# The test for the fast path by partition and a matmul, and the state's small matmuls in two bursts

## The chip, the cores and the metric

One core of a Trainium2 chip runs the whole program. The metric is the device time of one execution in microseconds; the runs shown are three executions of the kernel before, with their median. The profile is one more execution, taken by the hardware profiler, with a time of its own. Engines are named as the profile names them: PE (TensorE) with PEld for its weight loads, DVE (VectorE), ACT (ScalarE), POOL (GpSimd), SP (the engine that issues most DMAs).

## The reference, cut to what matters

```python
x = A_x                                                   # [1, 2048, 1024], 32 heads of 32
g = sigmoid((x * gate_w).sum(-1, keepdims=True))
# A: linear attention
q, k, v = heads(x @ A_wqkv)
phi = lambda t: where(t > 0, t + 1, exp(t)) + 1e-6
pq, pk = phi(q), phi(k)
kv = einsum("bhsd,bhse->bhde", pk, v)
z = einsum("bhsd->bhd", pk)
a = (einsum("bhqd,bhde->bhqe", pq, kv) / (einsum("bhqd,bhd->bhq", pq, z)[..., None] + 1e-6)) @ A_wo
# B: each position attends to 8 positions, 2 apart, back from its own
q, k, v = heads(x @ B_wqkv)
b = (softmax(masked(q . k[idx]) * 32 ** -0.5) @ v[idx]) @ B_wo
return g * a + (1 - g) * b
```

(`heads` splits into 32 heads; the heads are joined again ahead of each output product.)

## The kernel before

All engines run one static order. `Prog.op` records each operation with its reads, writes, a cost in the planner's units and a priority; `Prog.schedule` lays the operations out engine by engine, always the ready one of lowest priority; `emit` writes that order with semaphores. Each engine works strictly in its order, so an operation that waits holds all behind it on that engine. PSUM has eight banks; `Pool.next` deals them out, and PE may write a bank again when ACT and DVE have read it.

The program goes through these stages:

- `v` of part B, then `k` and `q` of part B for all positions (`kT`, `qT`), up to about 175 us. While they come, `top` keeps a running maximum and minimum of all values in `mx` on DVE.
- `k` of part A: for each of 16 tiles of 128 positions two groups of eight matmuls, and `phi` (ACT exponent L1374, DVE L1375 and L1377) writes `pk`. Between the groups, one in five `slot` calls starts a `fill`: the sliding attention of 114 positions in one burst of small matmuls (L1518 for scores, and in the same burst L1542, probabilities times `v`, of the fill before), then ACT's exponent into `E`, DVE's mask (L1528), reciprocals (L1553) and products into `ao` (L1554), which go out to `oB_hbm` and come back transposed into `qT`.
- `mT`, the product of x with `pk` (L1712), with the other fills between. POOL adds up `z`, which takes a trip of its own through HBM (`zr`, `zb`).
- `state` (L1682): `kvT`, 32 small products of `w` with `mT` by head, each over 8 chunks: 256 matmuls of 128x32 by 32 columns (L1690) in one operation. Then `query` (`pq`, L1745), `fold` (L1730: `kvT` times A's output weights, 16 matmuls of 32x32 tiles, evicted into `ws[5]`, which lies in `kT`), and `scaled` (the division by `den`, L1758 to L1768).
- `output` (L1771): 16 tiles; each half adds part B (`qT` times `Bo` in `ws[0]`) and part A (`aT` times the folded weights) in one bank, which ACT or DVE scale and evict.

The fast path is right only within bounds on the values: the largest |q| or |k| of part B, squared, must be at most 40/32, and a measure of the gate at most 1e17. `mx4` holds for each partition the maximum, the minimum and the gate's measure. `fast_ok` (L1613) turns this into one number, `flag`: it negates the minimum (L1615), sends the 128x3 values to `mx_hbm` (L1617), reads them back as one row of 384 in one partition (L1618), takes the maximum of each kind (L1619) and tests it (L1622 to L1625). Its DVE operations get a priority 40 later than their place. In `tail`, every engine waits for `flag`, loads it and branches to the fast or the general path: SP after eight of the output DMAs, the others at or near the end of their work.

Of the kernel before, what the change touches and what calls it, by code (L numbers as in the profile page):

```python
# [15 lines left out]
DH = 32  # L16
# [1103 lines left out]
def build_kernel(nc, A_x, A_wqkv, A_wo, B_x, B_wqkv, B_wo, gate_w, out):  # L1120
# [61 lines left out]
    banks = [Bank(i) for i in range(8)]  # L1182
    vB_hbm = nc.dram_tensor("vB_hbm", [S, H * 33], BF16)
    oB_hbm = nc.dram_tensor("oB_hbm", [S, D], BF16)
    MX = [("M", 0, 1, None)]
    ZH = [("M", 1, 2, None)]
    z_hbm = nc.dram_tensor("z_hbm", [128, 8], BF16)
    mx_hbm = nc.dram_tensor("mx_hbm", [128, 3], F32)

    def hb(p0, p1, half):  # L1190
        return [("H%d" % half, p0, p1, None)]
# [9 lines left out]
    aT = SB([128, 8, S], BF16, "aT", at=ws[1].lo)  # L1201
    mT = SB([128, 8, 1024], BF16, "mT", at=ws[3].lo)
    ws += [Half(kT, 0), Half(kT, HS)]
    ones = SB([128, 128], BF16, "ones")

    FILLS = [(2 * 57 * b, 57, (0 if b == 0 else 7, 7)) for b in range(8)] + [(2 * 57 * 8, 56, (7, 8))]
    KINDS = ((57, (0, 7)), (57, (7, 7)), (56, (7, 8)))
# [8 lines left out]
    denr = Ring([SB([128, H], F32, "den%d" % i) for i in range(2)])  # L1216
    mx4 = SB([128, 3], F32, "mx4")
    pick = SB([128, 2], F32, "pick")
    mx1 = SB([1, 3], F32, "mx1")
    flag = SB([1, 1], I32, "flag")  # L1220
    zs = SB([128, 16], F32, "zs")
    zc = SB([128, 8], BF16, "zc")
# [11 lines left out]
    mtmp = [SB([128, 2, 57], BF16, "mt%d" % i, at=vr.t[2].lo + 256 * i) for i in range(2)]  # L1234
    base[0] = max(base[0], top_)
    prodr = Ring([SB([128, 1024], F32, "prod%d" % i, at=Er.t[0].lo + 4096 * i) for i in range(2)])
    mxr = SB([1, 384], F32, "mxr")

    ph = base[0]
    mx = [SB([128, 1024], BF16, "mx%d" % i, at=ph + 2048 * i) for i in range(2)]  # L1240
# [23 lines left out]
    def plan(seen):  # L1264
# [29 lines left out]
        def C(eng, fn, cost, writes, reads=()):  # L1294
            return P.op(eng, fn, cost, reads=reads, writes=writes, prio=-1)

        C("pool", lambda e: e.memset(ones[:], 1.0), 0.1, [ones.all()])
        C("dve", lambda e: e.memset(pick[:, :], 0.0), 0.1, [pick.all()])
        P.ops[-1].prio = 1100
        for i in range(4):  # L1300
# [91 lines left out]
        def move(dst, src, n, bank, reg, scale=None, reads=()):  # L1392

            if scale is None:
                fd = lambda e: e.tensor_copy(dst, src())  # L1395
                fa = lambda e: e.activation(dst, src(), ACT.Copy)  # L1396
            else:
                fd = lambda e: e.tensor_scalar(dst, src(), scale, None, op0=ALU.mult)  # L1398
                fa = lambda e: e.activation(dst, src(), ACT.Copy, scale=scale)
            P.op("any", {"act": fa, "dve": fd}, {"act": act(n) + (0.1 if reads else 0.0), "dve": dps(n)}, reads=[bank.iv] + list(reads), writes=[reg])  # L1400
# [207 lines left out]
                    P.op("dve", lambda e: e.reciprocal(gm[:, :], gm[:, :]), 0.25, reads=[gm.all()], writes=[gm.all()])  # L1608
        after(6, lambda: top_end(0, ALU.max))
        after(11, lambda: top_end(1, ALU.min))  # L1610
        flag_op = []

        def fast_ok():  # L1613
            first = len(P.ops)
            P.op("dve", lambda e: e.tensor_scalar(mx4[:, 1:2], mx4[:, 1:2], -1.0, None, op0=ALU.mult), 0.1, reads=[mx4.part((1, 2))], writes=[mx4.part((1, 2))])  # L1615

            P.op("sp", lambda e: e.dma_start(mx_hbm[:, :], mx4[:, :]), 0.4, reads=[mx4.all()], writes=[MX], chan="mxo", lat=0.5)  # L1617
            P.op("sp", lambda e: e.dma_start(mxr[0:1, :], mx_hbm.rearrange("p i -> (p i)")[None, :]), 0.1, reads=[MX], writes=[mxr.all()], chan="mxi", lat=0.5)  # L1618
            P.op("dve", lambda e: e.tensor_reduce(mx1[:, :], mxr[:, :].rearrange("o (p i) -> o i p", i=3), AX.X, ALU.max), dps(384), reads=[mxr.all()], writes=[mx1.all()])  # L1619
            small = [mx1.all()]  # L1620
            for o, i0, i1 in ((ALU.max, 0, 1), (ALU.mult, 0, 0)):
                P.op("dve", lambda e, o=o, i0=i0, i1=i1: e.tensor_tensor(mx1[:, i0:i0 + 1], mx1[:, i0:i0 + 1], mx1[:, i1:i1 + 1], o), 0.1, reads=small, writes=small)  # L1622
            P.op("dve", lambda e: e.tensor_scalar(mx1[:, 0:1], mx1[:, 0:1], 40.0 / DH, None, op0=ALU.is_le), 0.1, reads=small, writes=small)
            P.op("dve", lambda e: e.tensor_scalar(mx1[:, 2:3], mx1[:, 2:3], 1e17, None, op0=ALU.is_le), 0.1, reads=small, writes=small)  # L1624
            flag_op.append(P.op("dve", lambda e: e.tensor_tensor(flag[:, :], mx1[:, 0:1], mx1[:, 2:3], ALU.mult), 0.1, reads=small, writes=[flag.all()]))  # L1625
            for o in P.ops[first:]:
                o.prio += 40 if o.eng == "dve" else 0

        after(12, fast_ok)
        xnv = A_x[0].rearrange("(r p e) d -> e p r d", p=128, e=2)  # L1630
# [48 lines left out]

        z_add(3)  # L1680
        n_masks = [len(masks)]
        def state():  # L1682
            sb = main.next()

            def fn(e):
                for i in range(8):
                    for c in range(8):
                        for j in range(4):
                            h = 4 * i + j
                            last = e.matmul(sb.ap()[32 * j:32 * j + 32, i * 32:i * 32 + 32], ws[0][:, c, h * 32:(h + 1) * 32], mT[:, c, h * 32:(h + 1) * 32],  # L1690
                                            start=(c == 0), stop=(c == 7), tile_position=(0, 32 * j))
                return last
            P.op("pe", fn, 2.1, mode="c", reads=[ws[0].all(), mT.all()], writes=[sb.iv], name="kv")
            move(kvT[:, :, :].rearrange("p i d -> p (i d)"), lambda: sb.ap(0, 256), 256, sb, kvT.all())

        wait_w = [True]

# [32 lines left out]
        def fold(gq, jh):  # L1730
            bs = [main.next() for _ in range(4)]
            w = ws[5].part((4 * gq, 4 * gq + 4), (jh * 512, jh * 512 + 512))

            def fn(e):
                for a in range(4):
                    for j in range(4):
                        b = (a + j) % 4
                        last = e.matmul(bs[j].ap()[32 * b:32 * b + 32, :], kvT[32 * j:32 * j + 32, 4 * gq + b, :], ws[5][32 * j:32 * j + 32, 4 * gq + b, jh * 512:(jh + 1) * 512],  # L1738
                                        start=True, stop=True, tile_position=(32 * j, 32 * b))
                return last  # L1740
            P.op("pe", fn, 0.45, mode="r", reads=[kvT.all(), w], writes=[b.iv for b in bs], name="fold")
            for j in range(4):
                move(ws[5][:, 4 * gq + j, jh * 512:(jh + 1) * 512], bs[j].ap, 512, bs[j], ws[5].part((4 * gq + j, 4 * gq + j + 1), (jh * 512, jh * 512 + 512)))

# [56 lines left out]
        while later:  # L1801
            slot(0)
        main = Pool(banks)
        state()
        load_w(0, 0, Bo, 0, 54)
        load_w(0, 1, Bo, 512, 55)
        query(1, 0)
        query(1, 1)
        fold(0, 0)
        query(2, 0)  # L1810
# [7 lines left out]
        query(4, 0)  # L1818
        query(4, 1)
        fold(1, 1)  # L1820
        for t in range(NT):
            if t + 2 < NT:
                scaled(t + 2)
            output(t)
            if t + 5 < NT:
                queries(t + 5)

        P.schedule()
        return P, flag_op[0], [max(o.end for o in P.held[n]) for n in range(len(takes))]

    best = None
    seen = None
# [76 lines left out]
```

## Time and profile before

| | |
|---|---|
| three runs, median (lowest to highest) | 489.47 us (488.1 to 489.69) |
| the profiled execution's own time | 488.77 us |
| its span, from the first to the last instruction | 486.9 us |
| PE busy | 470.9 us, 97% of the span |
| PE weight loads (PEld) | 227.3 us, 47% |
| DVE busy | 316.5 us, 65% |
| ACT busy | 129.9 us, 27% |
| POOL busy | 40.2 us, 8% |
| mean granted clock of PE | 0.996 |

The profiled execution takes 1.9 us more than its span, which lies around the instructions. Busy shares are averages over stages with different limits; where PE waits is read from the timeline of a place. In a timeline a row gives start and duration in us, the engine, the line and operation, written and read names, shape and count, and in brackets how long the engine stood idle before and what ended that. SPq is SP's queue of DMA issues. PE's ends are modelled, and some of its records are missing (x39 for 40).

### The profile page before, as it was taken

What the parts mean: (1) busy time and instruction counts of PE and PEld (TensorE: products, weight loads), DVE (VectorE), ACT (ScalarE), POOL (GpSimd) and SP (SyncE); (2) the same over time, 40 slices, a digit from 0 to 9 for tenths busy, and PEclk for the clock granted to TensorE, in tenths of its full rate; (3) what the DMA queues carried; (4) which work ended last, traced back from release to release, by engine and by line L of the source; (5) the groups of instructions that cost most, each with busy time, mean ns of one, the idle gap of its engine ahead of it and who ended that gap; (6) DMA issues with size and microseconds to landing.
All of it is one profiled execution on the core that took longest, in us unless ns stands there. A gap on an engine that the chain in (4) does not pass through costs nothing.

```text
span 486.9 us, 9582 instructions
## 1 busy us (share of the span) xinstructions
PE 470.9 (97%) x4115; PEld 227.3 (47%) x4162; DVE 316.5 (65%) x555; ACT 129.9 (27%) x174; POOL 40.2 (8%) x40
## 2 busy tenths in 40 slices
PE   9999999999999999987999999889999999999997
PEld 7444444444454445543444544434444444444444
DVE  2121276799878888865866465479977777767522
ACT  1111111212344445643534333134221000011000
POOL 3000000000000000000058651100000000000000
PEclk9999999999999999998999999999999999999999
DMA  9999995233012362274234876661142111141111
GB/s 234 211 200 308 361 360 155 77 96 108 24 43 58 77 172 70 73 174 109 55 64 127 192 168 114 181 195 25 44 108 66 43 44 44 44 80 51 45 43 47
DMA packets 95116, 57.09 MB, mean 117 GB/s; under 512 B 55385, under 2 KB 88538, under 8 KB 95066
## 3 DMA queue, kind: packets, MB, share of 16 engines
q1 hardware_dynamic: 94234, 55.61, 43.6%
q10 hardware_dynamic: 832, 0.79, 0.5%
q8 instruction: 34, 0.56, 0.5%
q14 instruction: 16, 0.13, 0.1%
HBM read 30.56 MB, written 12.72 MB: 89 GB/s over the span
## 4 chain that ended last, share of the span: by engine, by line
PE 95%; DMA 2%; issue 2%; DVE 1%
PE ps_all L1368 55%; PE ps_all L1783 23%; PE ps_all L1712 11%; PE ps_all L1518 2%; PE ps_all L1542 2%; DMA mx_hbm<-mx 1%; PE ps_all L1404 1%; DMA mxr<-mx_hbm 1%; PE ps_all L1690 1%; PE ps_all L1738 0%; DVE mx L1619 0%; DVE pk L1377 0%; DVE o L1398 0%; DVE e L1375 0%; DVE ao L1554 0%
## 5 line engine op out<-in xcount | busy, mean ns | idle before, releaser
L1368 PE MATMUL ps_all<-w,xT 128*128 128x512 bf16 x500 | 112.2, 383 | 5.1 <-DVE mx L1624 2.4
L1368 PE MATMUL ps_all<-xT,w 128*128 128x512 bf16 x500 | 110.2, 379 | 1.2 <-issue 0.8
L1368 PEld LDWEIGHTS ps_all<-w,xT 128*128 128x128 bf16 x512 | 49.8, 99 | 64.6 <-DVE mx L1624 2.9
L1368 PEld LDWEIGHTS ps_all<-xT,w 128*128 128x128 bf16 x512 | 49.6, 98 | 59.2
L1374 ACT ACTIVATE e<-ps_all 128x512 bf16<-128x512 f32 x64 | 38.2, 597 | 130.5 <-PE ps_all L1368 128.2
L1783 PE MATMUL ps_all<-w,qT 128*128 128x512 bf16 (+1 forms) x256 | 59.9, 372 | 0.5 <-issue 0.2
L1783 PE MATMUL ps_all<-kT,aT 128*128 128x512 bf16 (+1 forms) x258 | 60.0, 372 | 0.3
L1368 PE MATMUL ps_all<-kT,xT 128*128 128x512 bf16 x254 | 57.5, 379 | 0.3 <-issue 0.3
L1712 PE MATMUL ps_all<-pk,xn 128*128 128x512 bf16 x249 | 55.0, 379 | 1.1 <-issue 1.1
L1395 DVE CAST vst<-ps_all 128x512 bf16<-128x512 f32 x16 | 11.1, 694 | 44.7 <-PE ps_all L1368 44.7
L1783 PEld LDWEIGHTS ps_all<-w,qT 128*128 128x128 bf16 x264 | 25.7, 98 | 29.6 <-issue 0.2
L1783 PEld LDWEIGHTS ps_all<-kT,aT 128*128 128x128 bf16 x264 | 25.8, 98 | 29.4
L1375 DVE TENSOR_SCALAR e<-e 128x512 bf16<-128x512 bf16 x64 | 18.8, 295 | 31.2 <-ACT e L1374 30.9
L1398 DVE TENSOR_SCALAR o<-ps_all,gm 128x512 bf16<-128x512 f32 (+1 forms) x28 | 20.5, 731 | 28.1 <-PE ps_all L1783 28.1
L1368 PEld LDWEIGHTS ps_all<-kT,xT 128*128 128x128 bf16 x256 | 24.7, 98 | 30.0 <-issue 0.5
L1712 PEld LDWEIGHTS ps_all<-pk,xn 128*128 128x128 bf16 x256 | 24.5, 98 | 28.8
L1523 ACT ACTIVATE E<-ps_all 128x1824 bf16<-128x1824 f32 (+1 forms) x18 | 30.4, 1688 | 23.4 <-PE ps_all L1542 19.0
L1676 POOL TENSOR_TENSOR zacc<-zacc,pk 128x1024 f32<-128x1024 f32 x15 | 32.8, 2187 | 12.1 <-DVE E L1528 11.2
L1554 DVE TENSOR_TENSOR ao<-ps_all,rs 128x896 bf16<-128x896 f32 (+1 forms) x36 | 24.5, 682 | 0.2
L1396 ACT ACTIVATE kT<-ps_all 128x512 bf16<-128x512 f32 x25 | 14.4, 598 | 34.7 <-PE ps_all L1368 34.7
L1396 ACT ACTIVATE vst<-ps_all 128x512 bf16<-128x512 f32 x16 | 9.6, 600 | 49.5 <-PE ps_all L1368 49.5
L1377 DVE SCALAR_TENSOR_TENSOR p<-ps_all,e 128x512 bf16<-128x512 f32 x32 | 22.0, 689 | 0.7
(66 smaller groups left out, 349.0 us busy)
## 6 DMA issues: line engine op xcount, KB each, us to landing
v<-vB_hbm SPq DMA_DIRECT2D x36, 132.0 KB, 3.3
vB_hbm<-vst SPq DMA_DIRECT2D x32, 132.0 KB, 5.5
w<-in_B_wqkv_dram SPq DMA_DIRECT2D x4, 1024.0 KB, 8.5
xt<-in_A_x_dram SPq DMA_DIRECT2D x16, 256.0 KB, 4.8
w<-in_A_wqkv_dram SPq DMA_DIRECT2D x4, 1024.0 KB, 9.6
xn<-in_A_x_dram SPq DMA_DIRECT2D x8, 512.0 KB, 5.8
out_dram<-o SPq DMA_DIRECT2D x15, 256.0 KB, 2.0
oB_hbm<-ao SPq DMA_DIRECT2D x32, 114.0 KB
```

The costliest lines, as they stand in the source:

```text
L1368: last = e.matmul(bank.ap(), lhs(dc), rhs(dc), start=(dc == 0), stop=(dc == 7))
L1374: P.op("act", lambda e: e.activation(e_[:, :], bank.ap(), ACT.Exp), act(512), reads=[bank.iv], writes=[e_.all()])
L1375: P.op("dve", lambda e: e.tensor_scalar(e_[:, :], e_[:, :], 1.0, 1e-6, op0=ALU.min, op1=ALU.add), 0.25, reads=[e_.all()], writes=[e_.all()])
L1377: P.op("dve", lambda e: e.scalar_tensor_tensor(out=dst, in0=bank.ap(), scalar=0.0, in1=e_[:, :], op0=ALU.max, op1=ALU.add), dps(512), read ...
L1395: fd = lambda e: e.tensor_copy(dst, src())
L1396: fa = lambda e: e.activation(dst, src(), ACT.Copy)
L1398: fd = lambda e: e.tensor_scalar(dst, src(), scale, None, op0=ALU.mult)
L1523: P.op("act", lambda e: e.activation(E[:, 0:32 * nq].rearrange("p (j q) -> p j q", j=4), ps[:, 4:8, 0:8 * nq], ACT.Exp), act(32 * nq), rea ...
L1554: P.op("dve", lambda e, i0=i0, i1=i1, src=src: e.tensor_tensor(o_[:, :, i0:i1, :], src(0, 32), rs[:, :, i0:i1, None].to_broadcast([128, 2, ...
L1676: P.op("pool", lambda e, t=t: e.tensor_tensor(zacc[:, :], zacc[:, :], pkS[:, t, :], ALU.add), 2.2, reads=[src, zacc.all()], writes=[zacc.a ...
L1712: last = e.matmul(bank.ap(), tl[:, t, cs:cs + 128], pkS[:, t, r * 512:(r + 1) * 512], start=(t == 0), stop=(t == NT - 1))
L1783: last = e.matmul(bank.ap(0, f1 - f0), lh[:, k, t * 128:(t + 1) * 128], w[:, k, f0:f1], start=(first and k == 0), stop=(not first and k == 7))
```

## The change

The test: each partition now tests its own three values, in six DVE operations on 128x1 columns of `mx4`, and writes 1 or 0 to `okp`, a bf16 column. `all_ok`, called after the last `fold`, multiplies `okp` with a column of ones on PE, which adds the 128 results into one PSUM value, and DVE compares it with 127.5 into `flag`. `mx_hbm`, the row `mxr`, `mx1` and the unused `ones` go. All operations of the test now have the later priority.

The state: `state(n)` makes one half (four of the eight column blocks, 128 matmuls), with an eviction of its own; it depends on the half of `ws[0]`, `mT` and `kvT` that it uses, and comes on PE right after the operation recorded before it. `query(1, 0)` moves between the halves, and the loads of `Bo` into `ws[0]` are recorded after the second. A `fold` depends on its half of `kvT`.

```diff
-    mx_hbm = nc.dram_tensor("mx_hbm", [128, 3], F32)
-    ones = SB([128, 128], BF16, "ones")
-    mx1 = SB([1, 3], F32, "mx1")
+    okp = SB([128, 1], BF16, "okp")
-    mxr = SB([1, 384], F32, "mxr")
-        C("pool", lambda e: e.memset(ones[:], 1.0), 0.1, [ones.all()])
...
         def fast_ok():
             first = len(P.ops)
-            P.op("dve", lambda e: e.tensor_scalar(mx4[:, 1:2], mx4[:, 1:2], -1.0, None, op0=ALU.mult), 0.1, reads=[mx4.part((1, 2))], writes=[mx4.part((1, 2))])
-
-            P.op("sp", lambda e: e.dma_start(mx_hbm[:, :], mx4[:, :]), 0.4, reads=[mx4.all()], writes=[MX], chan="mxo", lat=0.5)
-            P.op("sp", lambda e: e.dma_start(mxr[0:1, :], mx_hbm.rearrange("p i -> (p i)")[None, :]), 0.1, reads=[MX], writes=[mxr.all()], chan="mxi", lat=0.5)
-            P.op("dve", lambda e: e.tensor_reduce(mx1[:, :], mxr[:, :].rearrange("o (p i) -> o i p", i=3), AX.X, ALU.max), dps(384), reads=[mxr.all()], writes=[mx1.all()])
...
+            w4 = [mx4.all()]
+            for o, i0, i1, sc in ((ALU.mult, 1, None, -1.0), (ALU.max, 0, 1, None), (ALU.mult, 0, 0, None), (ALU.is_le, 0, None, 40.0 / DH), (ALU.is_le, 2, None, 1e17)):
...
+            P.op("dve", lambda e: e.tensor_tensor(okp[:, :], mx4[:, 0:1], mx4[:, 2:3], ALU.mult), 0.1, reads=w4, writes=[okp.all()])
             for o in P.ops[first:]:
-                o.prio += 40 if o.eng == "dve" else 0
+                o.prio += 40
+
+        def all_ok():
+            bank = main.next()
+            P.op("pe", lambda e: e.matmul(bank.ap(0, 1)[0:1, :], okp[:, 0:1], one(1), start=True, stop=True), 0.06, reads=[okp.all()], writes=[bank.iv])
+            return P.op("dve", lambda e: e.tensor_scalar(flag[:, :], bank.ap(0, 1)[0:1, :], 127.5, None, op0=ALU.is_ge), 0.1, reads=[bank.iv], writes=[flag.all()])
...
-        def state():
+        def state(n):
...
-                for i in range(8):
+                for i in range(4 * n, 4 * n + 4):
...
-            P.op("pe", fn, 2.1, mode="c", reads=[ws[0].all(), mT.all()], writes=[sb.iv], name="kv")
-            move(kvT[:, :, :].rearrange("p i d -> p (i d)"), lambda: sb.ap(0, 256), 256, sb, kvT.all())
+            cols = (512 * n, 512 * n + 512)
+            P.op("pe", fn, 1.05, mode="c", reads=[ws[0].part((0, 8), cols), mT.part((0, 8), cols)], writes=[sb.iv], name="kv", after=[[o for o in P.ops if o.eng == "pe"][-1]])
+            move(kvT[:, 4 * n:4 * n + 4, :].rearrange("p i d -> p (i d)"), lambda: sb.ap(128 * n, 128 * n + 128), 128, sb, kvT.part((4 * n, 4 * n + 4), (0, 32)))
...
-        state()
+        state(0)
+        query(1, 0)
+        state(1)
         load_w(0, 0, Bo, 0, 54)
         load_w(0, 1, Bo, 512, 55)
-        query(1, 0)
         query(1, 1)
...
         fold(1, 1)
+        flag_op = all_ok()
```

On DVE, in the stage of `pk`, these rows stood around the reduce of the row that came back (numbers in names are those of the buffers; `mx_26_74` is `mx1`, `mxr_94` the row, `E_82` the probabilities):

```order
L1554 TENSOR_TENSOR ao_37_85<-ps_all,rs_84 128x2x448
L1553 RECIPROCAL rs_84<-ps_all 128x2x2
L1528 TENSOR_TENSOR E_82<-E_82,msk_12_60 128x1824
L1619 TENSOR_REDUCE mx_26_74<-mxr_94 1x3
L1554 TENSOR_TENSOR ao_37_85<-ps_all,rs_84 128x2x64
L1622 TENSOR_TENSOR mx_26_74<-mx_26_74 1x1
L1375 TENSOR_SCALAR e_30_78<-e_30_78 128x512
L1622 TENSOR_TENSOR mx_26_74<-mx_26_74 1x1
L1375 TENSOR_SCALAR e_31_79<-e_31_79 128x512
L1623 TENSOR_SCALAR mx_26_74<-mx_26_74 1x1
L1377 SCALAR_TENSOR_TENSOR pk_56<-ps_all,e_30_78 128x512
L1624 TENSOR_SCALAR mx_26_74<-mx_26_74 1x1
```

At the same place of the changed kernel (lines are some five lower there, buffer numbers one lower):

```order
L1549 TENSOR_TENSOR ao_36_84<-ps_all,rs_83 128x2x448
L1548 RECIPROCAL rs_83<-ps_all 128x2x2
L1523 TENSOR_TENSOR E_81<-E_81,msk_11_59 128x1824
L1549 TENSOR_TENSOR ao_36_84<-ps_all,rs_83 128x2x64
L1370 TENSOR_SCALAR e_29_77<-e_29_77 128x512
L1372 SCALAR_TENSOR_TENSOR pk_56<-ps_all,e_29_77 128x512
L1370 TENSOR_SCALAR e_30_78<-e_30_78 128x512
L1372 SCALAR_TENSOR_TENSOR pk_56<-ps_all,e_30_78 128x512
```

The test's operations are gone from this place; they stand one round of the fills earlier, one or two at a time between the operations of `phi` (`mx_23_71` is `mx4`):

```order
L1372 SCALAR_TENSOR_TENSOR pk_56<-ps_all,e_29_77 128x512
L1612 TENSOR_TENSOR mx_23_71<-mx_23_71 128x1 x2
L1370 TENSOR_SCALAR e_31_79<-e_31_79 128x512
L1548 RECIPROCAL rs_83<-ps_all 128x2x14
L1372 SCALAR_TENSOR_TENSOR pk_56<-ps_all,e_31_79 128x512
L1549 TENSOR_TENSOR ao_37_85<-ps_all,rs_83 128x2x448
L1548 RECIPROCAL rs_83<-ps_all 128x2x2
L1523 TENSOR_TENSOR E_81<-E_81,msk_13_61 128x1792
L1549 TENSOR_TENSOR ao_37_85<-ps_all,rs_83 128x2x64
L1370 TENSOR_SCALAR e_30_78<-e_30_78 128x512
L1614 TENSOR_SCALAR mx_23_71<-mx_23_71 128x1
L1372 SCALAR_TENSOR_TENSOR pk_56<-ps_all,e_30_78 128x512
```

The negation (L1615 before, L1614 now) has kept its place. On PE, at the state, before (`w_4_52` is `ws[0]`, `kT_51` holds `ws[4]` and `ws[5]`, so rows of L1368 are `query` and rows of L1738 `fold`):

```order
L1368 MATMUL ps_all<-kT_51,xT_49 128x512 x16
L1690 MATMUL ps_all<-mT_58,w_4_52 32x32 x256
L1368 MATMUL ps_all<-kT_51,xT_49 128x512 x16
L1738 MATMUL ps_all<-kT_51,kvT_67 32x512 x16
L1368 MATMUL ps_all<-kT_51,xT_49 128x512 x16
```

And now:

```order
L1363 MATMUL ps_all<-kT_51,xT_49 128x512 x16
L1685 MATMUL ps_all<-mT_58,w_4_52 32x32 x128
L1363 MATMUL ps_all<-kT_51,xT_49 128x512 x8
L1685 MATMUL ps_all<-mT_58,w_4_52 32x32 x128
L1363 MATMUL ps_all<-kT_51,xT_49 128x512 x8
L1734 MATMUL ps_all<-kT_51,kvT_66 32x512 x16
L1363 MATMUL ps_all<-kT_51,xT_49 128x512 x16
```

One group of eight has moved between the halves; else PE's order is the same but for the flag's matmul ahead of the first output.

More of the change, by code (lines that the diff above doesn't have):

```diff
@@ L1184, in build_kernel @@
     oB_hbm = nc.dram_tensor("oB_hbm", [S, D], BF16)
-    MX = [("M", 0, 1, None)]
     ZH = [("M", 1, 2, None)]
     z_hbm = nc.dram_tensor("z_hbm", [128, 8], BF16)
-    mx_hbm = nc.dram_tensor("mx_hbm", [128, 3], F32)
     def hb(p0, p1, half):
@@ L1610, in plan @@
         after(11, lambda: top_end(1, ALU.min))
-        flag_op = []
         def fast_ok():
             first = len(P.ops)
[L1615 to L1625, printed above, removed]
-            for o in P.ops[first:]:
-                o.prio += 40 if o.eng == "dve" else 0
@@ new lines, in fast_ok @@
+            w4 = [mx4.all()]
+            for o, i0, i1, sc in ((ALU.mult, 1, None, -1.0), (ALU.max, 0, 1, None), (ALU.mult, 0, 0, None), (ALU.is_le, 0, None, 40.0 / DH), (ALU.is_le, 2, None, 1e17)):
+                if sc is None:
+                    P.op("dve", lambda e, o=o, i0=i0, i1=i1: e.tensor_tensor(mx4[:, i0:i0 + 1], mx4[:, i0:i0 + 1], mx4[:, i1:i1 + 1], o), 0.1, reads=w4, writes=w4)
+                else:
+                    P.op("dve", lambda e, o=o, i0=i0, sc=sc: e.tensor_scalar(mx4[:, i0:i0 + 1], mx4[:, i0:i0 + 1], sc, None, op0=o), 0.1, reads=w4, writes=w4)
@@ L1740, in fn @@
                 return last
-            P.op("pe", fn, 0.45, mode="r", reads=[kvT.all(), w], writes=[b.iv for b in bs], name="fold")
+            P.op("pe", fn, 0.45, mode="r", reads=[kvT.part((4 * gq, 4 * gq + 4), (0, 32)), w], writes=[b.iv for b in bs], name="fold")
             for j in range(4):
@@ L1828, in plan @@
         P.schedule()
-        return P, flag_op[0], [max(o.end for o in P.held[n]) for n in range(len(takes))]
+        return P, flag_op, [max(o.end for o in P.held[n]) for n in range(len(takes))]
     best = None
```

## The prediction

> **What bounds the kernel now.** I read the chain of work that ended last first, then the table of waits, then the timelines of the two places where PE stands still. The chain of the page:
>
> ```profile
> PE 95%; DMA 2%; issue 2%; DVE 1%
> PE ps_all L1368 55%; PE ps_all L1783 23%; PE ps_all L1712 11%; PE ps_all L1518 2%; PE ps_all L1542 2%; DMA mx_hbm<-mx 1%; PE ps_all L1404 1%; DMA mxr<-mx_hbm 1%; PE ps_all L1690 1%; PE ps_all L1738 0%; DVE mx L1619 0%; DVE pk L1377 0%; DVE o L1398 0%; DVE e L1375 0%; DVE ao L1554 0%
> ```
>
> TensorE sets the end: 95% of the chain is its matmuls, end to end. So time is to be had only where PE is not fed. The two DMAs of the maxima stand in the chain, and so do 2% of "issue", in which PE waited for nothing that the profile shows. The waits of PE, longest first (engine, line, what it waited for, us in total, times, longest):
>
> ```profile
> PE ps_all L1690 <- issue: 3.1, 1, 3.1
> PE ps_all L1368 <- DVE mx L1624: 2.4, 1, 2.4
> PE ps_all L1368 <- DVE pk L1377: 1.4, 1, 1.4
> ```
>
> These are three single events, and both parts of the change sit exactly on them. The timeline of PE around the maxima (start, duration, instruction, idle time before it):
>
> ```profile
> 203.83 0.59 PE L1518 MATMUL ps_all<-qx,kT 64*64 64x112 bf16 x32
> ...
> 213.59 0.60 PE L1518 MATMUL ps_all<-qx,kT 64*64 64x114 bf16 x32
> 214.03 0.67 PE L1542 MATMUL ps_all<-v,E 64*56 64x33 bf16 x64
> ...
> 217.97 3.63 PE L1368 MATMUL ps_all<-w,xT 128*128 128x512 bf16 x16 [1.44 <-DVE pk L1377]
> 224.01 5.31 PE L1368 MATMUL ps_all<-w,xT 128*128 128x512 bf16 x16 [2.41 <-DVE mx L1624]
> 229.26 0.60 PE L1518 MATMUL ps_all<-qx,kT 64*64 64x114 bf16 x32
> ...
> 239.13 0.60 PE L1518 MATMUL ps_all<-qx,kT 64*64 64x114 bf16 x32
> ```
>
> The L1518 burst and its L1542 half (1.1 us together) open a round, and five groups of eight matmuls follow. A round takes 9.76 us (203.83 to 213.59) or 9.87 us (229.26 to 239.13); the one between takes 15.67 us. **It is 5.85 us too long**: 1.44 and 2.41 us of idle time, and sixteen matmuls in 5.31 us where the row above has 3.63 us, 1.68 us more. The clock of that stretch, by the table of stretches (us, busy time and instructions of PE, PEld, DVE, ACT and POOL, granted clock, DMA share, GB/s):
>
> ```profile
> 224.80:228.30 3.50, 3.50 (x11) 1.22 (x8) 1.83 (x5) 0.60 (x1) 0.00 (x0) 0.51 0.77 179
> ```
>
> So 3.4 us ran at half clock right after the idle time. Why PE stood still, in the timeline of all engines:
>
> ```profile
> 203.11 0.15 DVE L1615 TENSOR_SCALAR mx<-mx 128x1 f32<-128x1 f32 x1
> ...
> 210.35 0.57 SPq L1617 DMA_DIRECT2D mx_hbm<-mx  x1
> ...
> 217.04 0.33 DVE L1553 RECIPROCAL rs<-ps_all 128x28 f32<-128x28 f32 x1 [2.41 <-PE ps_all L1368]
> 217.17 0.23 SPq L1618 DMA_DIRECT2D mxr<-mx_hbm  x1
> 217.29 0.63 DVE L1377 SCALAR_TENSOR_TENSOR pk<-ps_all,e 128x512 bf16<-128x512 f32 x1
> ...
> 218.91 1.08 DVE L1528 TENSOR_TENSOR E<-E,msk 128x1824 bf16<-128x1824 bf16 x1
> ...
> 221.90 0.65 DVE L1619 TENSOR_REDUCE mx<-mxr 1x3 f32<-1x384 f32 x1 [1.91 <-DMA mxr<-mx_hbm]
> ...
> 222.48 0.27 DVE L1554 TENSOR_TENSOR ao<-ps_all,rs 128x128 bf16<-128x128 f32 x1
> ...
> 222.75 0.28 DVE L1375 TENSOR_SCALAR e<-e 128x512 bf16<-128x512 bf16 x1
> ...
> 223.28 0.67 DVE L1377 SCALAR_TENSOR_TENSOR pk<-ps_all,e 128x512 bf16<-128x512 f32 x1
> ```
>
> The maxima are ready at 203.26, leave SP's queue at 210.35, and the row of 384 values is back only at 221.9. The reduce that needs it stands in DVE's order between the mask of `E` and the two `pk` that free PSUM banks; DVE waits 1.91 us, then does it, and PE waits behind.
>
> The other place, PE at the state:
>
> ```profile
> 313.45 1.95 PE L1690 MATMUL ps_all<-mT,w 128*32 128x32 bf16 x200
> 318.47 0.59 PE L1690 MATMUL ps_all<-mT,w 128*32 128x32 bf16 x56 [3.07 <-issue]
> 319.22 3.40 PE L1368 MATMUL ps_all<-kT,xT 128*128 128x512 bf16 x15 [0.16 <-issue]
> 322.55 0.43 PE L1738 MATMUL ps_all<-kT,kvT 32*32 32x512 bf16 x16
> ```
>
> PE runs 200 of 256 small matmuls, each with a weight load, and then stops inside the burst, with no semaphore to wait for. The DMA tables of 313.4 to 315.4 (first row) and of 315.4 to 318.47 (second) name the packets:
>
> ```profile
> q1 hardware_dynamic: 1287, 0.32, 97.1%
> q8 instruction: 1, 0.02, 2.2%
> 311.54 3.15 SPq L1476 DMA_TRANSPOSE qT<-oB_hbm  x2
> ```
>
> While the burst ran, small packets filled the engines to 97% and no instruction packet of q8 passed; in the stall one did. I read the stall as **PE out of instructions**: 400 in 1.95 us, and the next block stuck behind the transposes of `oB_hbm` that SP issued from 311.54 on (third row, from the timeline).
>
> **The change part by part.** *The trip through HBM* (two DMAs, a reduce of 0.65 us, five 1x1 operations) goes, and with it the only DMA wait in that part of DVE's order. What is late next? Without L1619 the `pk` behind the mask would end at 219.99 + 0.27 (`ao`) + 0.28 (`e`) + 0.67 = 221.2 us, before the sixteen matmuls from 217.97 end (221.6). So the 2.41 us go whole, and the half clock that followed them. The 1.44 us come from DVE starting the reciprocal at 217.04, though PE's burst of 213.59 is drawn as over by 214.7; that start falls within 0.13 us of the landing of `mx_hbm` (SP's next issue, 217.17). In no other round does this lag appear, and no other has this transfer, so I let it go too: **-5.85 us**. Bounds: -4.41 if the lag stays, -2.41 if the half clock stays as well.
>
> The new test is six operations of the form of 203.11, 0.15 us each, five more than the old one had there. DVE is nearly full next to them, but has gaps on both sides:
>
> ```profile
> 204.57 0.29 DVE L1375 TENSOR_SCALAR e<-e 128x512 bf16<-128x512 bf16 x1 [0.65 <-ACT e L1374]
> ...
> 212.66 0.29 DVE L1375 TENSOR_SCALAR e<-e 128x512 bf16<-128x512 bf16 x1 [0.77 <-ACT e L1374]
> ```
>
> They hide there: 0, and 5 x 0.15 = 0.75 us if they did not. On SP the wait for `mx_hbm` goes; behind it stood only loads of `v`, which come earlier.
>
> *The sum by a matmul*: one 1x1 matmul on PE before the first output, in its plain mode, and one DVE operation behind it. The trace has no such matmul; it lies between one of L1690 (0.01 us) and a whole fold burst (0.43 us). I take **+0.1 us**, nearer the small one, since one instruction is what is added. The flag is read late in every engine's order, far behind 335 us, so its lateness costs nothing.
>
> *The state in two bursts* of 128, with one group of `query(1)` moved between them: eight matmuls, 1.73 us, by a round ((9.76 - 1.1) / 5). The stream reaches the missing block after the same number of instructions, up to some 16: 128 small matmuls (1.25 us), a group (1.73), 64 small ones (0.62), with about 0.4 for the changes of mode (0.16 idle behind a burst in the row of 319.22, and about as much ahead of one), so at 313.45 + 4.0 = 317.5. If the block comes at 318.47 as now, a stall of about 1 us is left, then 64 small ones and one group where now 56 and two follow: 1.73 - 0.08 = **-1.65 us**. The bounds: 0 if the block comes later by as much as the group covers; -2.7 if it is there in time (9.10 us from 313.45 to the fold become 2 x 1.25 + 2 x 1.73 + 0.4 = 6.4). I take -1.65, since the transposes that the block waits for are triggered by PE's last bursts and move with them. [...]
>
> What else moves with it: the loads of `Bo` into `ws[0]` must wait for the second burst, and DVE evicts `kvT` in two pieces.
>
> ```profile
> 319.15 2.34 SPq L1346 DMA_DIRECT2D w<-in_B_wo_dram  x2
> 319.15 0.42 DVE L1395 CAST kvT<-ps_all 128x256 bf16<-128x256 f32 x1 [1.04 <-PE ps_all L1690]
> ...
> 326.00:334.00 8.00, 7.84 (x65) 3.29 (x65) 7.98 (x15) 4.83 (x9) 0.00 (x0) 1.00 0.23 59
> ...
> 334.87 0.69 DVE L1395 CAST kT<-ps_all 128x512 bf16<-128x512 f32 x1 [0.50 <-PE ps_all L1738]
> ...
> w<-in_B_wo_dram SPq DMA_DIRECT2D x2, 1024.0 KB, 7.0
> ```
>
> Their issue stays where it is against the burst's begin (its end moves by 0.1 us); they land some 7 us later (last row, from the page) and are first read after 334.9, behind the last fold, so 1.65 us less room does not matter. DVE is busy for 7.98 of 8.0 us during the folds, yet waits 1.04 us for PE before `kvT` and 0.50 us before the last fold's eviction: it follows PE, and follows earlier. If it could not, the folds would give back up to 1.65 - 0.50 = 1.15 us.
>
> Sum, against the profiled execution's own 488.77 us (span 486.9): 488.77 - 5.85 + 0.1 - 1.65 = **481.4**. The median of the runs, 489.47, is 0.7 above that execution; I forecast **481.7**, the sum with half of that.
>
> **The rivals.**
> *The lag of 217.04 stays*, because the loads of x and of weights that run there cause it and not the transfer of the maxima.
>
> ```profile
> 210.00:215.00 5.00, 4.84 (x114) 2.69 (x114) 2.90 (x7) 2.73 (x4) 0.00 (x0) 1.00 1.08 214
> ```
>
> For: the DMA engines are full there (share 1.08). Against: no other loaded stretch shows it. +1.44: 483.1.
> *The half clock stays*: 2.41 us of idle time would not be its cause, since the 3.07 us at 315.4 were followed by none. For: that difference. Against: the two idle times lie right before it, in one round. +1.68: 483.4. [...]
> *The state does not gain*, because the block is later by the group's length: +1.65, 483.4. *Or it is in time*: -1.05, 480.7.
> *The change doesn't do what it says*: another wait of DVE holds PE in that round; then only the state gains, 487.5. The order has no DMA wait left there, so this needs an unseen one.
> *Slower*: the second state bank and the flag's bank shift the round-robin of PSUM banks in the output loop. If each tile were dealt a bank that DVE evicts behind its two pairs of `prod` and `den`,
>
> ```profile
> 338.80 2.35 DVE L1758 TENSOR_TENSOR prod<-p,zb 128x1024 f32<-128x1024 bf16 x2
> ...
> 341.07 2.34 DVE L1759 TENSOR_REDUCE den<-prod 128x32 f32<-128x1024 f32 x2
> ```
>
> an eviction would come 4.7 + 0.7 us late against some 3.5 us of one output half (sixteen matmuls; fifteen take 3.40 in the row of 319.22): 1.9 us a tile, 16 tiles, 30 us, so 512. It decides from 0.47 us a tile, which eats the whole gain. Against: with eight banks one comes round after seven other claims, 12 us and more.
>
> **How the numbers follow.** Forecast 0.56; lag stays 0.13; half clock stays 0.06; state without gain 0.08; state in time 0.09; change without its first effect 0.05; slower 0.03. The range takes in the forecast, the four small rivals, the lag and the idle state together (481.7 + 1.44 + 1.65 = 484.8) and below it the block in time with the flag at no cost: 480.2 to 484.9. By this count it holds 0.9; I trust it for about 0.8, since a sum of single stalls has no row for what comes new. A measurement of this kernel tells about 0.3%, 1.5 us, from no change: faster by more 0.94, within 0.03 (a part of the 487.5 case, which lies near the edge), slower 0.03.
>
> **What would show it.** Right: the rounds between bursts of the pk phase are all 9.8 us; PE's waits have no DVE row of over 1 us; the clock holds 1.0 there; the state shows two bursts, the second broken after about 64 matmuls by an "issue" of about 1 us. Wrong: an idle time of 1.4 us behind the burst near 214.7 (the lag), a stretch at 0.5 with no idle time before it (the clock), a stall still near 3 us or a new one at L1518, or PE waiting for DVE during the folds.

## The result and the profile after

| | before | after |
|---|---|---|
| median of six runs each, side by side | 488.86 us (486.94 to 491.48) | 481.32 us (480.46 to 482.03) |
| ratio, 95% interval | | 0.984 [0.981, 0.987] |
| profiled execution, span | 488.77, 486.9 us | 480.46, 478.6 us |

The change is faster by 1.6%, 7.5 us by the medians; 481.7 was forecast. The chain of work of the page after, by engine and by line:

```profile
PE 98%; issue 1%; DVE 0%
PE ps_all L1363 57%; PE ps_all L1779 23%; PE ps_all L1708 11%; PE ps_all L1513 2%; PE ps_all L1537 2%; PE ps_all L1399 1%; PE ps_all L1685 1%; PE ps_all L1734 0%; DVE o L1393 0%; PE ps_all L1621 0%
```

Both transfers of the maxima have left the chain with their 2%, and so has 1% of "issue". Lines are some five lower than before: the bursts of the fills are L1513 and L1537, the big products L1363, the state L1685. The table of PE's waits (us in total, times, longest), without its rows of PE's start and of single 0.2 us:

```profile
PE ps_all L1363 <- issue: 2.1, 13, 0.2
PE ps_all L1708 <- issue: 1.1, 7, 0.2
PE ps_all L1685 <- issue: 0.9, 1, 0.9
```

Of the three single waits of before, the two for DVE are gone, and that of the state is 0.9 in place of 3.1 us. The rest are short waits of about 0.16 us; those in the rows below stand behind a burst of small matmuls. PE's timeline at the place of the maxima, with three rounds of the fills:

```profile
202.88 0.59 PE L1513 MATMUL ps_all<-qx,kT 64*64 64x112 bf16 x32
...
212.64 0.60 PE L1513 MATMUL ps_all<-qx,kT 64*64 64x114 bf16 x32
...
213.91 8.58 PE L1363 MATMUL ps_all<-w,xT 128*128 128x512 bf16 x39 [0.16 <-issue]
222.42 0.60 PE L1513 MATMUL ps_all<-qx,kT 64*64 64x114 bf16 x32
...
232.19 0.60 PE L1513 MATMUL ps_all<-qx,kT 64*64 64x114 bf16 x32
```

The three rounds take 9.76, 9.78 and 9.77 us, and the forty matmuls of the middle one stand in one row with nothing between them. DVE at the same place:

```profile
210.13 0.16 DVE L1615 TENSOR_TENSOR okp<-mx 128x1 bf16<-128x1 f32 x1
...
213.83 0.33 DVE L1548 RECIPROCAL rs<-ps_all 128x28 f32<-128x28 f32 x1 [0.16 <-PE ps_all L1537]
...
215.71 1.08 DVE L1523 TENSOR_TENSOR E<-E,msk 128x1824 bf16<-128x1824 bf16 x1
...
217.22 0.69 DVE L1372 SCALAR_TENSOR_TENSOR pk<-ps_all,e 128x512 bf16<-128x512 f32 x1
```

The test is done at 210.3. The reciprocal starts 1.19 us after the burst's begin at 212.64; before it was 3.45 us (213.59 to 217.04): the lag is gone. Behind the mask, `pk` follows with no wait. The clock there, from the table of stretches (us, busy time of PE, PEld, DVE, ACT, POOL, granted clock, DMA share, GB/s):

```profile
219.00:222.50 3.50, 3.50 (x24) 1.45 (x24) 2.42 (x5) 2.14 (x3) 0.00 (x0) 1.00 0.42 106
```

The 24 are 17 of the large matmuls and 7 of the small ones of the next burst; in the stretch of before, 11 large ones ran at 0.51. Last, PE at the state:

```profile
306.52 1.32 PE L1685 MATMUL ps_all<-mT,w 128*32 128x32 bf16 x128
308.00 1.67 PE L1363 MATMUL ps_all<-kT,xT 128*128 128x512 bf16 x7 [0.16 <-issue]
309.60 0.66 PE L1685 MATMUL ps_all<-mT,w 128*32 128x32 bf16 x64
311.21 0.66 PE L1685 MATMUL ps_all<-mT,w 128*32 128x32 bf16 x64 [0.94 <-issue]
312.03 1.67 PE L1363 MATMUL ps_all<-kT,xT 128*128 128x512 bf16 x7 [0.16 <-issue]
313.63 0.43 PE L1734 MATMUL ps_all<-kT,kvT 32*32 32x512 bf16 x16
```

The second burst stops after 64 matmuls for 0.94 us. With the group of eight between (one record of it is missing), that is after 128 + 8 + 64 = 200 matmuls: the place in the instruction stream at which the one burst stopped before.

So the 8.3 us between the two spans split up, stretch by stretch:

| stretch of PE | before, us | after, us | gained |
|---|---|---|---|
| up to the first round shown | 203.83 | 202.88 | 0.95 |
| the three rounds | 35.30 | 29.31 | 5.99 |
| from there to the state's first matmul | 74.32 | 74.33 | 0 |
| from there to the first fold | 9.10 | 7.11 | 1.99 |
| from there to the first output | 12.37 | 12.46 | -0.09 |
| the outputs and the drain behind them | 152.0 | 152.5 | -0.5 |

The 0.95 us arise at the program's start: the warm-up matmuls run at 10 in a microsecond up to about 6 us before and up to about 4 us now, and the weight load of PE's first product stands at 6.82 and 5.87 us. The edit does not touch the warm-up, and `state_only` with its old test begins the burst of the middle round at 212.60 us, as early as the kernel after (212.64; before 213.59); so this is no part of the change. The -0.09 is the flag's matmul. The 0.5 us lie behind the last product. 8.3 less the start and the drain is 7.9; the medians say 7.5.

### The profile page after: what moved, and what is told of

Its sections match the earlier page's. It is cut to its first block, busy times and chain, and to the rows that moved or that the text cites. A ratio compares the mean times of both kernels' runs of the same rounds, so it can differ in the third digit from the quotient of the medians.

```text
span 478.6 us, 9580 instructions
## 1 busy us (share of the span) xinstructions
PE 467.9 (98%) x4115; PEld 226.0 (47%) x4163; DVE 316.3 (66%) x556; ACT 130.0 (27%) x174; POOL 40.1 (8%) x39
## 4 chain that ended last, share of the span: by engine, by line
PE 98%; issue 1%; DVE 0%
PE ps_all L1363 57%; PE ps_all L1779 23%; PE ps_all L1708 11%; PE ps_all L1513 2%; PE ps_all L1537 2%; PE ps_all L1399 1%; PE ps_all L1685 1%; PE ps_all L1734 0%; DVE o L1393 0%; PE ps_all L1621 0%
## 5 line engine op out<-in xcount | busy, mean ns | idle before, releaser
L1363 PE MATMUL ps_all<-w,xT 128*128 128x512 bf16 x500 | 110.2, 379 | 1.3 <-issue 0.8
L1363 PE MATMUL ps_all<-xT,w 128*128 128x512 bf16 x500 | 110.2, 379 | 1.2 <-issue 0.8
L1363 PEld LDWEIGHTS ps_all<-xT,w 128*128 128x128 bf16 x512 | 49.6, 98 | 59.2
L1363 PEld LDWEIGHTS ps_all<-w,xT 128*128 128x128 bf16 x512 | 49.6, 98 | 58.9
L1363 PE MATMUL ps_all<-kT,xT 128*128 128x512 bf16 x253 | 57.4, 379 | 0.5 <-issue 0.5
L1363 PEld LDWEIGHTS ps_all<-kT,xT 128*128 128x128 bf16 x256 | 24.7, 98 | 29.8 <-issue 0.5
```

The costliest lines, as they stand in the source:

```text
L1363: last = e.matmul(bank.ap(), lhs(dc), rhs(dc), start=(dc == 0), stop=(dc == 7))
```

## The experiments

Ratios are to the kernel before, run side by side with each group of kernels (its medians there: 487.92, 490.17 and 488.8 us, so compare gains across groups with care); a range beside a median is that of all runs. Theory of the prediction: DVE's wait for the row costs PE idle time, half clock follows that, the lag belongs to the transfer of the maxima, and the state's stall is a block of instructions that comes late and can be covered by other work.

### The test alone: `test_only`

The new test, with the state of before.

```diff
-        state(0)
-        query(1, 0)
-        state(1)
+        state()
         load_w(0, 0, Bo, 0, 54)
         load_w(0, 1, Bo, 512, 55)
+        query(1, 0)
         query(1, 1)
```

> The new test with the old state (256 matmuls in one burst, one eviction). Theory (the two parts are separate stalls of PE): the rounds of the pk stage all take 9.8 us, the state keeps its stall near 3 us after 200 matmuls; about 5.9 us faster than the kernel before, 483.0. Rival (the state's stall is a consequence of the earlier disturbance): the state's stall is gone too, 481.3 or less. Rival (the lag of 1.44 us belongs to the loads of x and weights): a gap of 1.4 us is left in the round after the tenth burst in some profile, 484.4.

484.14 us (482.32 to 485.27), ratio 0.990 [0.987, 0.994], before 487.92: 3.8 us gained where about 5.9 were expected. No wait of PE for DVE is over 0.2 us and the state's stall is as before, 3.08 us, so the two parts are separate stalls. PE's timeline there, and the stretch behind the stall:

```profile
307.25 2.10 PE L1685 MATMUL ps_all<-mT,w 128*32 128x32 bf16 x200
312.43 0.61 PE L1685 MATMUL ps_all<-mT,w 128*32 128x32 bf16 x56 [3.08 <-issue]
...
312.60:316.00 3.40, 3.07 (x63) 1.44 (x49) 1.55 (x2) 0.00 (x0) 0.00 (x0) 0.50 0.46 126
```

The half clock is not gone: it now follows the state's stall. Nine of ten runs show a mean granted clock of 0.996 or less; the one with 1.0 is the fastest, 482.32.

### The state alone: `state_only`

The kernel before, with the state in two bursts.

```diff
-        state()
+        state(0)
+        query(1, 0)
+        state(1)
         load_w(0, 0, Bo, 0, 54)
         load_w(0, 1, Bo, 512, 55)
-        query(1, 0)
         query(1, 1)
```

> The old test with its trip through HBM, the state in two bursts. Theory: one round of the pk stage takes 15 to 16 us again, with an idle time behind the reduce of the returned row; the second burst of the state breaks after 64 matmuls for about 1 us; about 2.0 us faster than before, 486.9. If the late end of the tenth burst (1.44 us) is caused by the transfer of the maxima it is seen again here; if it was a single event it is not, and the idle time ahead of the reduce's release is longer by as much, with the same total.

485.87 us (483.76 to 486.9), ratio 0.995 [0.992, 0.998]: 2.05 us gained. In its profile (a run of 483.76, clock 1.0) the lag and the wait for the row are back, but the round takes 13.30 us (212.60 to 225.90), not the 15 to 16 expected; the state's second burst breaks after 64 matmuls for 1.42 us. PE's timeline in that round:

```profile
217.24 3.63 PE L1368 MATMUL ps_all<-w,xT 128*128 128x512 bf16 x16 [1.70 <-DVE pk L1377]
222.34 3.63 PE L1368 MATMUL ps_all<-w,xT 128*128 128x512 bf16 x16 [1.48 <-DVE mx L1624]
```

Here the sixteen matmuls behind the second gap run at full speed. So gaps of 1.70 and 1.48 us brought no half clock in this run; six of the ten runs have a clock of 0.996 or less. The two parts alone gain 3.8 + 2.05 = 5.8 us and together 7.5. The 1.7 us between is the size of one window of half clock, which either part's remaining stall could bring. The intervals of the two (1.5 us each way) are too wide to prove this; the clocks of the runs point the same way.

### A transfer that nothing waits for: `dead_trip`

The kernel after, with both transfers of the maxima at their old place in SP's queue; nothing reads the row.

```diff
+            P.op("dve", lambda e: e.tensor_copy(mxc[:, :], mx4[:, :]), 0.1, reads=w4, writes=[mxc.all()])
+            P.op("sp", lambda e: e.dma_start(mx_hbm[:, :], mxc[:, :]), 0.4, reads=[mxc.all()], writes=[MX], chan="mxo", lat=0.5)
+            P.op("sp", lambda e: e.dma_start(mxr[0:1, :], mx_hbm.rearrange("p i -> (p i)")[None, :]), 0.1, reads=[MX], writes=[mxr.all()], chan="mxi", lat=0.5)
```

> The changed kernel with the two transfers of the maxima put back at their old places in SP's order; nobody reads the row that comes back. Theory A (the transfer itself makes the end of the tenth burst come late): DVE's reciprocal behind the tenth burst starts some 2 us after the burst's drawn end and PE idles about 1.4 us; 482.7. Theory B (only DVE's wait for the row cost time, and the late end was a single event): no idle time of over 0.5 us in that round, same time as the changed kernel, 481.3.

482.44 us (481.82 to 482.81), ratio 0.983 [0.978, 0.989]. The lag returns, first in DVE's timeline, then in PE's:

```profile
216.04 0.33 DVE L1552 RECIPROCAL rs<-ps_all 128x28 f32<-128x28 f32 x1 [2.12 <-PE ps_all L1367]
...
216.97 7.08 PE L1367 MATMUL ps_all<-w,xT 128*128 128x512 bf16 x32 [1.15 <-DVE pk L1376]
```

The round takes 11.10 us, 1.3 more than in the kernel after. The ratio, 0.983 against 0.984, does not show it; the reading rests on the profiles. The lag stands in all three with both transfers (before, `state_only`, `dead_trip`: PE waits 1.44, 1.70 and 1.15 us for `pk` there), and without a write of the maxima DVE goes on 1.19 (after), 1.18 (`after_again`) and 1.19 us (`two_between_again`) after that burst begins. So the lag belongs to these transfers, though no operation waits for them; the loads of x and of weights are the same in both kernels. The clock stays 1.0.

### Idle time without a transfer: `hold`

The kernel after, with one long reduce on DVE behind the mask of that round. It reads a tile of zeros seven times, and nothing uses its result.

```diff
+            if len(masks) == 10:
+                P.op("dve", lambda e: e.tensor_reduce(held[:, :], hold[:, :][:, None, :].to_broadcast([128, 7, 512]), AX.X, ALU.max), 0.01, reads=[hold.all()], writes=[held.all()], prio=mk.prio + 0.001, after=[mk])
```

> The changed kernel with one reduce over 3584 elements (about 3.9 us of DVE, no transfer) at the place of the old reduce, behind the tenth mask. Theory (the half clock follows from PE's idle time): PE idles about 2.6 us once and a stretch of 3.4 us at half clock may follow, 1.7 us more; 3.9 + clock, so 484 without and 485.6 with it. Rival (the half clock came with the transfers or the DMA load): only the idle time, and no half clock in any run, 484.

485.39 us (484.01 to 488.31), ratio 0.993 [0.990, 0.996] where the kernel after has 0.984: some 4 us of the gain are given back. PE's timeline, and the stretch behind the gap:

```profile
221.78 5.31 PE L1367 MATMUL ps_all<-w,xT 128*128 128x512 bf16 x16 [2.73 <-DVE pk L1376]
...
222.20:225.50 3.30, 3.30 (x9) 1.22 (x8) 1.71 (x4) 0.34 (x1) 0.00 (x0) 0.50 0.61 155
```

With no transfer of the maxima, the picture of before is back: one gap, then sixteen matmuls in the same 5.31 us. Nine of the ten runs show a clock of 0.996 or less, the tenth 0.998. Here half clock (0.50) followed 2.73 us of idle time of PE, and the transfer was not needed for it.

### Where the stall sits: `shift`

`test_only`, with 90 short warm-up matmuls at the start in place of 50 longer ones: as much time, 40 more matmuls with their weight loads.

```diff
-    WARM = 50
+    WARM = 90
-            P.op("pe", lambda e: e.matmul(banks[7].ap(0, 156), one(128), one(156), start=True, stop=True), 0.13, writes=[banks[7].iv], prio=-1)
+            P.op("pe", lambda e: e.matmul(banks[7].ap(0, 84), one(128), one(84), start=True, stop=True), 0.072, writes=[banks[7].iv], prio=-1)
```

> The new test with the old state, and 90 warm-up matmuls of 84 columns in place of 50 of 156: 80 more instructions ahead of all else on PE, about the same time. Theory (PE stops where a block of instructions ends): the state's stall moves from after 200 to after 160 matmuls. Rival (a limit within the burst, counted from its begin): it stays after 200. Time as the new test with the old state, 483.0, within 0.5.

483.37 us (481.54 to 487.47), ratio 0.985 [0.979, 0.990]; the profiled run is the slowest. PE's timeline, and two stretches of the clock:

```profile
299.93 0.20 PE L1537 MATMUL ps_all<-v,E 64*56 64x33 bf16 x2 [0.97 <-issue]
...
308.80 1.61 PE L1685 MATMUL ps_all<-mT,w 128*32 128x32 bf16 x160
315.29 0.96 PE L1685 MATMUL ps_all<-mT,w 128*32 128x32 bf16 x96 [4.87 <-issue]
...
314.30:317.70 3.40, 2.08 (x99) 1.44 (x101) 2.42 (x3) 0.00 (x0) 0.00 (x0) 0.50 0.05 15
317.70:321.10 3.40, 3.40 (x9) 1.21 (x8) 0.83 (x4) 0.60 (x1) 0.00 (x0) 0.50 1.01 315
```

The break moved from after 200 matmuls to after 160, by just the 40 that were put in 300 us earlier. So it is a place in the instruction stream, not a time or an operand. A burst of the fills now meets such a place too (299.93). The stall is longer here, and two windows of half clock follow.

### What the block waits for: `no_last_turn`

`test_only`, without the transposes of the last two tiles of part B's output, which SP issues ahead of the state. This kernel leaves out a part of the result: two tiles of the output come from other data.

```diff
                 turned[0] += 1
+                if t >= NT - 2:
+                    continue
```

> The new test with the old state, without the last two transposes of part B's output, so that two tiles of the output are computed from other data. Theory (the block waits behind these transposes in the DMA engines): the instruction packet comes about 1 us earlier against the begin of the state and the stall falls from about 3 us to 2 or less, 482.0. Rival (the block comes late whatever else is moved): the stall stays at 3 us, 483.0.

482.97 us (482.25 to 483.29), ratio 0.985 [0.980, 0.990]. PE's timeline:

```profile
307.39 1.80 PE L1687 MATMUL ps_all<-mT,w 128*32 128x32 bf16 x200
311.79 0.59 PE L1687 MATMUL ps_all<-mT,w 128*32 128x32 bf16 x56 [2.60 <-issue]
```

PE goes on 4.40 us after the burst's begin, against 5.18 in `test_only`. But the kernel after, unchanged, differs by nearly as much between two profiles (4.69 us, and 5.41 in `after_again`), so it is not shown that the transposes cost the block these 0.78 us. What is shown is that it comes late without them: from 306 to 312.46 us SP issues no transfer, and PE still stands for 2.60 us. That the block was "stuck behind the transposes" is not borne out.

### More work between the bursts: `two_between`

The kernel after, with both groups of `query(1)` between the bursts.

```diff
         state(0)
         query(1, 0)
+        query(1, 1)
         state(1)
         load_w(0, 0, Bo, 0, 54)
         load_w(0, 1, Bo, 512, 55)
-        query(1, 1)
```

> The changed kernel with both groups of query(1) between the bursts of the state, not one. Theory (a block of instructions arrives some 4.7 us after the first burst's begin, and PE needs it 64 matmuls into the second): 1.73 us more work covers the 0.94 us of stall that are left, no issue gap of over 0.3 us in the state, 0.9 us faster than the changed kernel, 480.4. Rival (the gap is a pause that PE makes after some 400 small instructions, whatever the clock says): a gap of about 1 us stays in the second burst, 481.3.

479.63 us (479.3 to 479.8), ratio 0.982 [0.977, 0.988]. PE's timeline:

```profile
306.81 1.32 PE L1685 MATMUL ps_all<-mT,w 128*32 128x32 bf16 x128
...
311.62 1.19 PE L1685 MATMUL ps_all<-mT,w 128*32 128x32 bf16 x128
312.75 0.43 PE L1734 MATMUL ps_all<-kT,kvT 32*32 32x512 bf16 x16
```

The second burst is one row; from the first matmul to the fold it takes 5.94 us. No pause is left, so the stall was no fixed pause after so many small matmuls but time that work can cover. The margin is thin: PE reaches matmul 200 at about 311.62 + 56 x 1.19 / 128 = 312.1, 5.3 us after the start, and in the other runs here PE went on after 4.4 to 6.5 us.

### Which transfer makes the lag: `dead_write` and `wide_write`

`dead_trip` without the way back, so that only the write of 128 rows of 12 bytes is left; and the same write with rows of 512 bytes, of which the first 12 are the maxima.

```diff
-    mx_hbm = nc.dram_tensor("mx_hbm", [128, 3], F32)
+    mx_hbm = nc.dram_tensor("mx_hbm", [128, 128], F32)
...
-    mxc = SB([128, 3], F32, "mxc")
+    mxc = SB([128, 128], F32, "mxc")
...
-            P.op("dve", lambda e: e.tensor_copy(mxc[:, :], mx4[:, :]), 0.1, reads=w4, writes=[mxc.all()])
+            P.op("dve", lambda e: e.tensor_copy(mxc[:, 0:3], mx4[:, :]), 0.1, reads=w4 + [mxc.all()], writes=[mxc.all()])
```

> The changed kernel with only the first transfer put back, 128 rows of 12 bytes from SBUF to HBM, read by nobody. Theory (this transfer makes the end of the tenth burst come late): the gap of about 1.3 us behind that burst is there as with both transfers. Rival (the late end needs the read back, or SP's wait for the landing): all rounds 9.8 us, as the changed kernel, 481.3.

> As the one before, with rows of 512 bytes in place of 12 (the same 128 rows, 64 KB). Theory (the small rows do it): no gap behind the tenth burst, all rounds 9.8 us. Rival (any write from SBUF to HBM at that place, behind the loads, does it): the same gap of about 1.3 us.

481.91 us (480.88 to 482.76), ratio 0.986 [0.980, 0.991], and 481.41 us (480.08 to 482.44), ratio 0.984 [0.979, 0.989]; the times do not tell them apart, the profiles do. DVE's reciprocal and SP's next load of `v`, which waits for the same burst, with the small rows:

```profile
215.33 0.33 DVE L1551 RECIPROCAL rs<-ps_all 128x28 f32<-128x28 f32 x1 [1.27 <-PE ps_all L1540]
...
215.32 0.45 SPq L1507 DMA_DIRECT2D v<-vB_hbm  x1
```

And with rows of 512 bytes:

```profile
214.64 0.33 DVE L1553 RECIPROCAL rs<-ps_all 128x28 f32<-128x28 f32 x1 [0.16 <-PE ps_all L1542]
...
214.63 1.93 SPq L1509 DMA_DIRECT2D v<-vB_hbm  x1
```

The bursts begin at 213.03 and 213.45, so both engines go on after 2.3 us with small rows and 1.2 with wide ones. That DVE and SP go at the same moment says that the end of PE's burst is seen late, not that DVE is slow; PE itself goes on to the next matmuls at once, 214.29. The round is 10.25 us with small rows and 9.78 with wide ones, and PE's gap with small rows is 0.30 us, not the 1.3 expected: the write alone makes only a part of the lag. With the way back as well it is larger (`dead_trip`: 216.04 - 212.88 = 3.2). Each is one profile. Why such a write delays it was not found.

### Both once more, side by side: `after_again` and `two_between_again`

The kernel after and `two_between`, unchanged, five rounds each.

> The changed kernel once more, beside the version with both groups between the bursts: 481.3, clock near 1.0 in nearly all runs.

> Both groups of query(1) between the bursts, once more beside the changed kernel: about 1.2 us faster than it (5.94 us from the state to the fold in the profile against 7.11), 480.1.

481.21 us (480.26 to 481.64), ratio 0.984 [0.980, 0.988], and 480.11 us (479.66 to 480.91), ratio 0.982 [0.978, 0.986]. The second bursts of the two, in PE's timelines:

```profile
312.31 0.66 PE L1685 MATMUL ps_all<-mT,w 128*32 128x32 bf16 x64 [1.64 <-issue]
...
311.72 1.20 PE L1685 MATMUL ps_all<-mT,w 128*32 128x32 bf16 x128
```

From the state's begin to the fold it is 7.83 and 5.87 us. The same kernel that had 0.94 us of stall in one profile has 1.64 in the next; `two_between` has none in either. Its ten runs lie at 479.3 to 480.91, the twelve of the kernel after at 480.26 to 482.03, so it is the fastest kernel here, by about 1.1 us where the two ran together, with a small overlap.

## Why the prediction was right

**The test, -5.85 us: 5.99 in the profile.** "The 2.41 us go whole" and "I let it go too", of the lag, both held: no wait for DVE is left, and `dead_trip` brings the lag back without any reader of the row. That refutes the rival in which the loads of x and weights alone cause it. `wide_write` points to the small rows, of which the prediction knew nothing. In the sum, 5.85 is the round's difference; the pieces named, 1.44, 2.41 and 1.68, add up to 5.53, and 0.32 has no name. The bound of -2.41 counts the one gap alone; with the lag and the half clock both left, 5.85 would come down to 2.73.

**The half clock.** The rival (idle time of 2.41 us is not its cause) fell with `hold`, which makes the same picture with a DVE operation alone: half clock followed 2.41 us (before) and 2.73 us (`hold`). How the 3.07 us at the state, which brought none, differ from them can be read from the same traces. The clock on record in the trace of before is full for 218.45 us, half for 3.413 and full for 259.41: 64, 1 and 76 periods of 3.413 us. These are stretches of before on that grid, two about the maxima and two about the state (us, busy time of PE, PEld, DVE, ACT, POOL, granted clock, DMA share, GB/s):

```profile
221.44:224.85 3.41, 1.00 (x5) 0.41 (x5) 2.95 (x13) 1.54 (x2) 0.00 (x0) 1.00 0.18 58
224.85:228.26 3.41, 3.41 (x9) 1.22 (x8) 1.74 (x5) 0.60 (x1) 0.00 (x0) 0.50 0.80 184
...
313.60:317.01 3.41, 1.80 (x200) 1.63 (x188) 1.11 (x3) 0.55 (x1) 2.00 (x1) 1.00 0.83 162
317.01:320.42 3.41, 1.79 (x62) 1.20 (x64) 2.37 (x3) 0.00 (x0) 0.00 (x0) 1.00 0.06 14
```

The 2.41 us fall into one period, in which PE works for 1.00 us, and the next runs at 0.50. The 3.07 us are cut in two by the grid, PE works for 1.80 and 1.79 us and is idle for 1.61 us in each part, and no half clock follows. In `test_only` half clock holds from 312.60 to 316.00, so the 3.08 us that end at 312.43 lie in the one period ahead of it (0.33 us of work). In before, up to the last product, the periods with the most idle time behind the 2.41 us have 1.61, 1.61 and 1.59 us, and none of these is followed by half clock. No run moved the grid on purpose, so this is read and not tested. By it, that the stall of 3.07 us brought none was one execution's place on that grid.

The sizes of these terms were in part luck. The idle times of 1.44 and 2.41 us are those of one execution; in `state_only` the same gaps are 1.70 and 1.48 us, and the round, with no half clock, is 3.5 us too long and not 5.85. On the other side the prediction gave one window of 1.68 us to the maxima alone: of the 43 runs of the kernel before beside these experiments 42 show a clock of 0.997 or less, and 23 of them 0.993 or less, which is the clock of the profile of `shift` with its two windows; in `test_only` the window sits behind the state's stall. The mean of the 43 is 0.993, by which I estimate some 3 us lost to half clock in a run. So the idle time was taken too large and the half clock too small, and the two errors made up for each other.

**The state, -1.65 us: -1.99 in the first profile.** The form is as forecast: two bursts, the second broken after 64 by a stall of about 1 us. In that profile the block came 4.69 us after the start where 5.02 was assumed, and 0.33 us is the difference of the two. It is the best of the seven profiles with one group between the bursts: their stalls are 0.94 to 1.93 us, and from the state's begin to the fold they gain 1.0 to 2.0 us on the 9.10 of before, 1.5 in the middle one. So the term stands within the spread of the block's arrival. `shift` shows that PE stops at a fixed place in the stream and `two_between` that other work covers the wait. The step on what holds the block back is not borne out: without the last transposes it is still late, and what makes it late stays open. The burst of 256 small matmuls stopped for 2.60 to 4.87 us in all four profiles that have it (before, `test_only`, `shift`, `no_last_turn`).

**The flag's matmul, +0.1: +0.09**, from the first fold to the outputs. Banks in the output loop did not matter: from its first weight load to its last product that stage takes 148.7 us in both. The price of 0.75 us for the test's extra operations on DVE was not paid.

**What the sum left out**: the start of PE's first products, 0.95 us earlier, and a drain 0.5 us longer at the end, in the one profiled execution. With the 0.34 us of the state and 0.14 of the rounds they make -0.9, by which it came out at 480.46 and not at the 481.4 worked out against it; the median, 481.32, is 0.4 from the forecast.

## What to carry over

Where one engine is 97% busy, look for its few long waits by name: three of them (3.07, 2.41 and 1.44 us) and the slow clock behind one of them (0.51) were the whole gain here, and each could be priced from its rows. A price from one profile is one execution's: look at the clocks of all runs beside it. Do not give the slow clock to one gap from one trace; price it for all gaps that may bring it: in `test_only`, with the gaps of the maxima gone, it followed the state's 3.08 us. Here a burst of 256 tiny matmuls stopped PE for 2.60 to 4.87 us at a fixed place in its stream, and sixteen large matmuls put ahead of that place left no pause (`two_between`).

## What was not expected of the hardware

- The window of half clock of before is 3.41 us long and made sixteen matmuls 1.68 us longer; it begins after 64 periods of its own length at full clock. Half clock followed gaps of PE of 2.41 us (before), 2.73 us (`hold`) and 3.08 us (`test_only`), but not the pair of 1.70 and 1.48 us (`state_only`), the 3.07 us of the state (before, 1.61 us in each of two periods), nor the 2.60 us (`no_last_turn`, clock 1.000; how the grid cuts them is not shown). Behind 4.87 us (`shift`) came two.
- A write of 128 rows of 12 bytes, which nothing waits for, went with a signal of PE's burst that came about 1.1 us later than with rows of 512 bytes (2.30 us after the burst's begin in `dead_write`, 1.19 in `wide_write`); with its way back it was about 2.0 us later (3.16, `dead_trip`; one profile each).
- PE stopped, as I read it for want of instructions, after exactly 400 of the state's stream (200 matmuls with their weight loads: before, `test_only`, `no_last_turn`), or after 320 when 80 instructions were added far ahead (`shift`), and went on 4.4 (`no_last_turn`) to 6.5 us (`shift`) after the burst's begin.
